# A linear-attention recurrence feeding a bilinear feed-forward block on one core: even tokens scaled by the odd token's alpha, token order restored at the product, one store per block, and new instruction orders

## The chip, the core and the metric

The kernel runs on one core of a Trainium2 chip. The core has a matrix engine (TensorE, "PE"; its weight loads are listed as "PEld"), a vector engine (VectorE, "DVE"), a scalar engine (ScalarE, "ACT"), a general engine (GpSimd, "POOL") and a queue engine (SyncE, "SP"). Each runs its own list of instructions in order and waits on semaphores for the others. 16 DMA engines move data between device memory and the core's on-chip memory; transfers are issued from the SP, POOL and ACT queues. [...]

The metric is the device time of one execution in microseconds (us).

## The reference

Attention first, over 4 batches, 8 heads, 768 tokens and a head width of 48, with one state matrix per batch and head:

```python
for t in range(S):
    state = alpha[:, :, t, :, None] * state + np.einsum('bhd,bhe->bhde', k[:, :, t], v[:, :, t])
    y[:, :, t] = np.einsum('bhd,bhde->bhe', q[:, :, t], state)
```

Its output, 3072 tokens of 384 features, goes through the feed-forward block:

```python
a = x @ w_a          # 384 -> 1536
b = x @ w_b          # 384 -> 1536
return (a * b) @ w_out   # 1536 -> 384
```

## The kernel before, in words

**Tiles.** The work is cut into six chunks. Chunk c holds two batches (units u = 0 and 1) and 256 consecutive tokens of each. A partition holds a pair of neighbouring tokens: r = 0 is the even one, r = 1 the odd one. The pairs split into two groups g of 64 partitions (`HC`).

**Attention of a chunk.** alpha, k, q and v are loaded (`load`). ACT takes the logarithm of alpha (`logs`, line 553), DVE adds the two logarithms of a pair (`pairs`, line 559), and a matmul with a triangular matrix sums them along the pairs of a group (`cum` in chunk 0, `cum2` in the others). The sum is the decay exponent of the odd token. For the even token DVE subtracts the odd token's logarithm (`even`, line 601). `expo` (line 610) makes four exponentials per unit on ACT: beta and its inverse, for odd and for even tokens. DVE multiplies k by the inverse and q by beta (`mul`, line 614). The products are transposed, on PE in chunks 0 and 1 (`turn`, then the copies `turned`), by DMA in the others (`turn_dma`). Then `scores` (line 722), the masking `masked` (line 727) on DVE, the state update (`state_pe`, line 693, and `state`), and the output `inner` and `carried` (both line 738), all in 64x64 tiles. `evac` (line 773) copies a unit's output to `xT`, which holds features on partitions and tokens along the row. Within a block of 128 columns the even tokens come first and then the odd ones.

**Feed-forward of a chunk.** For each of 12 slices f of the hidden width, `ff` (line 789) makes a and b in three matmuls each, for all 512 tokens ("*") or for the 256 of one unit ("0", "1"; `HALVES` takes every other block of 128 columns). ACT copies a out of PSUM (`ff_as`, line 795) and DVE multiplies it by b (`ff_prod`, lines 802 and 805). `ff_o` (line 812) multiplies four blocks m of 128 tokens by w_out, `ff_out` (lines 817 and 819) copies the result, and `store` (line 826) writes it with two DMAs: the 64 rows of even tokens and the 64 of odd ones, each to every other row of the output.

**Order.** Nothing is scheduled automatically. The string `PROGRAM` lists the steps one after another: `chunk: step arguments`. Each engine executes its own steps in that order, so that a waiting instruction holds up everything behind it on its engine, and a DMA waiting at the head of a queue holds up the DMAs behind it. A letter at the end names the engine (V is DVE, S ACT, P POOL, Y SP), a digit the PSUM bank. `K` is state_pe, `k` state, `C` turn, `Ce` turned, `D` scores, `M` masked, `SB` and `SA` carried, `Y` inner, `X` evac, `v` the cast of v, `W` and `Wo` weight loads, `T` turn_dma. `warm` issues matmuls on zeros (line 570) between the first steps. `gate` and `gatet` are one-element copies on POOL that wait for a transfer, so that POOL's loads behind them are issued only then. In chunk 0 the first step of the feed-forward follows the evacuation of unit 0, and the second half of the attention, `Y 1`, comes after it:

```python
0: k 1 1 V; as 1 0; Y 1; SA 1; b 1 0 5; X 1 S; pr 1 0; as 0 0
```

Of the kernel before, what the change touches and what calls it, by code (L numbers as in the profile page):

```python
# [17 lines left out]
0: c1; warm 70 0; cz 0 V; cs 0 V  # L18
0: ld a 0 Y; ld k 0 Y; ld q 0 Y; ld a 1 Y; ld k 1 Y; cs 1 V; ld q 1 Y; gate a 0; ln 0; ld v 0 P; cm 0; cm 1; l2 0 V; A 0 1; warm 48 0; le 0; E 0 b1
0: E 0 i1; cz 1 V; W a 0 256; E 0 i0; W b 0 256; mk 0 V; ln 1; ld v 1 P  # L20
1: ld a 0 P
0: E 0 b0; l2 1 V
1: ld k 0 P
0: mq 0 V; A 1 0
1: ld q 0 P
0: warm 4 1; le 1; E 1 i1
1: ld v 0 P
0: C 0 0 1; dk 6; W a 256 768; E 1 b0; Ce 0 0 V; E 1 i0; W b 256 768; D 0 0 2; E 1 b1; v 0 V; warm 5 4; de; mk 1 V; W a 768 1536; C 0 1 0; K 0 6
0: W b 768 1536; Ce 0 1 S; mq 1 V; warm 11 1
1: ld a 1 P  # L30
0: k 0 0 V; C 1 0 4
1: ld k 1 P
0: M 0 0; SB 0 0
1: ld q 1 P
0: C 1 1 5; Ce 1 0 S
1: ld v 1 P
0: k 0 1 V; D 0 1 2; Ce 1 1 S; Wo 0 6; M 0 1; D 1 0 6; warm 16 4; Wo 6 12; v 1 S; M 1 0
2: ld a * P
0: K 1 4; Y 0; SA 0; k 1 0 V
2: ld k * P  # L40
0: SB 1 6; D 1 1 2; X 0 S; M 1 1
2: ld q * P
1: ln 0
0: a 1 0 0; a 0 0 1
2: ld v * P
0: k 1 1 V; as 1 0; Y 1; SA 1; b 1 0 5; X 1 S; pr 1 0; as 0 0
1: l2 0 V
0: a 5 0 2
1: H 0 S
0: a 3 0 4; as 5 0; a 4 1 5  # L50
1: L 0 V
0: b 0 0 1; as 3 0; a 4 0 6; pr 0 0; a 5 1 7; a 2 0 3; as 4 1; b 5 0 2; b 3 0 0; pr 5 0; b 4 1 4; pr 3 0; as 5 1; b 5 1 2; pr 4 1; as 4 0; b 4 0 7
0: a 2 1 1; as 2 0; pr 4 0; a 1 1 4; pr 5 1; b 2 1 0
1: A2 0 5
0: as 2 1; a 3 1 2
1: le 0; E 0 i1
0: b 3 1 7; b 2 0 6; as 1 1; pr 2 1; a 7 * 3
1: E 0 i0
0: pr 2 0; a 10 * 1; as 3 1
1: mk 0 V; E 0 b1  # L60
0: b 1 1 2; as 10 *; a 6 * 0; pr 3 1; pr 1 1
1: E 0 b0
0: a 0 1 5
1: v 0 V
0: as 7 *; b 11 * 4
1: mq 0 V
0: as 6 *; b 10 * 6; b 7 * 3
1: ln 1
0: pr 10 *; a 11 * 7; pr 7 *; as 0 1; b 6 * 0
1: l2 1 V  # L70
0: as 11 *
1: C 0 0 1
0: pr 6 *
1: H 1 S
0: a 9 * 3
1: Ce 0 0 S; L 1 V
0: b 0 1 2
1: dk 6
0: pr 11 *; as 9 *; pr 0 1
1: D 0 0 4  # L80
0: b 9 * 1
1: de; M 0 0; A2 1 7; C 0 1 6; E 1 i1
0: pr 9 *
1: K 0 2; E 1 b1
0: a 8 * 0
1: k 0 0 V; le 1
0: b 8 * 5
1: k 0 1 V; E 1 b0
0: o 3 0 1; as 8 *
1: mq 1 V; E 1 i0  # L90
0: o 0 0 3; pr 8 *
1: Ce 0 1 S
0: o 2 0 0
1: mk 1 V; SB 0 6; D 0 1 4; C 1 0 2; M 0 1
0: o 0 1 -; o 2 1 -; ot 0 S; o 3 1 -; ot 2 V
1: Ce 1 0 V
0: st 2 Y
1: Y 0; SA 0
0: ot 3 S
1: v 1 V; D 1 0 0  # L100
0: st 3 Y
1: K 1 4; X 0 S; M 1 0; C 1 1 3
2: ln *
1: b 3 0 2; a 1 0 6; Ce 1 1 V; b 11 0 1; a 3 0 0; k 1 0 V
0: o 1 0 7
1: as 3 0
2: l2 * V
1: as 1 0; b 1 0 0; k 1 1 V
0: o 1 1 -
2: H * S  # L110
1: pr 3 0; a 0 0 5; pr 1 0
0: ot 1 S
1: a 11 0 4
2: L * V
1: b 0 0 2; as 0 0; a 5 0 0; as 11 0; a 8 0 3; pr 0 0; as 5 0; SB 1 6; D 1 1 4; pr 11 0; as 8 0; a 4 0 0; M 1 1
2: A2 1 2
1: as 4 0
2: A2 0 1; E 1 i1
1: b 4 0 3; a 2 0 0
2: le 1; E 0 b1  # L120
1: b 5 0 4
2: le 0; E 1 b1
1: b 8 0 5; Y 1; SA 1
2: E 1 i0
1: pr 4 0
2: dec
1: pr 8 0
2: E 0 b0
1: pr 5 0; a 6 0 3; X 1 S
2: mk 1 V  # L130
1: a 7 0 2; a 10 0 5; as 2 0; b 11 1 7
2: mq 0 V; E 0 i1
1: b 2 0 4
0: st 1 Y
1: b 6 0 0; as 7 0; b 7 0 1; as 6 0; pr 2 0; a 9 0 6
2: E 1 b0
1: pr 7 0; a 2 1 3
0: st 0 Y
1: a 0 1 2; pr 6 0; as 10 0; b 10 0 4
2: mq 1 V  # L140
1: as 2 1; b 2 1 0; as 0 1; b 0 1 5
2: v 1 S
1: a 9 1 1; pr 10 0
2: T 1
1: b 9 1 2; pr 0 1; a 5 1 3; as 9 1; pr 2 1; a 4 1 4
2: E 0 i0
1: b 4 1 1; pr 9 1; as 4 1; b 5 1 5
2: mk 0 V
1: a 11 1 0; as 9 0; b 9 0 4; as 5 1; a 3 1 2; pr 4 1
2: T 0  # L150
1: b 3 1 6; pr 9 0; as 3 1; a 1 1 1; pr 5 1; a 8 1 3; as 11 1; b 1 1 4; pr 3 1; as 1 1; a 10 1 0; pr 11 1; as 8 1; b 8 1 6; pr 1 1
2: v 0 S; gatet 1; D 1 0 2
3: ld a * P
1: pr 8 1; a 7 1 1
2: M 1 0
1: as 10 1
2: K * 6
1: as 7 1
3: ld k * P
1: b 6 1 5  # L160
2: k * 0 V
1: a 6 1 3; b 7 1 4
3: ld q * P
1: as 6 1
2: D 0 0 0
1: o 3 0 2
2: k * 1 V
3: ld v * P
1: pr 7 1; b 10 1 6; o 2 0 3; pr 6 1; pr 10 1
2: M 0 0; SB 1 4; D 1 1 6  # L170
1: o 2 1 -
3: ln *
2: M 1 1
1: o 1 0 1; ot 2 S
3: l2 * V
2: Y 1; SA 1
3: H * V
1: o 1 1 -
2: X 1 S
3: L * V  # L180
2: SB 0 6
1: ot 1 S
2: D 0 1 4
1: o 0 0 3
2: M 0 1
1: st 1 Y
3: A2 0 0; A2 1 1; E 0 b1
2: Y 0; SA 0
3: le 1; E 0 i1; le 0; E 1 b1
1: o 3 1 -  # L190
2: X 0 V
3: E 0 i0; dec; E 1 i1
1: o 0 1 -
3: v 0 V; E 1 i0; mk 0 V; E 0 b0
2: a 4 * 7
3: E 1 b0; mq 0 V
2: a 3 * 0
1: st 2 Y
2: a 0 * 5; as 3 *
3: mq 1 V  # L200
2: b 3 * 6
3: T 0
2: as 4 *
3: mk 1 V
2: a 6 * 1
3: v 1 S
2: b 4 * 4; pr 3 *
1: ot 0 S
2: b 0 * 7; as 6 *
1: st 0 Y  # L210
2: pr 4 *; a 1 * 3; as 0 *; b 6 * 6
1: ot 3 S
2: pr 0 *
3: T 1
2: as 1 *; a 9 * 5
1: st 3 Y
2: pr 6 *; b 1 * 2; as 9 *
3: D 0 0 0
2: pr 1 *
3: K * 6; M 0 0  # L220
2: b 11 * 5; b 2 * 2
3: k * 0 V
2: a 11 * 1
3: gatet 1
2: a 2 * 0
4: ld a * P
2: as 11 *
3: k * 1 V
2: b 9 * 4; as 2 *
4: ld k * P  # L230
2: b 7 * 3; pr 9 *; a 7 * 1; pr 11 *
4: ld q * P
2: a 8 * 6; as 7 *; pr 2 *; a 5 * 0
4: ld v * P
2: as 8 *; pr 7 *
3: D 1 0 4
2: as 5 *; a 10 * 7
3: M 1 0
2: b 8 * 1; as 10 *; b 5 * 2; pr 8 *
4: ln *  # L240
3: SB 1 6
2: pr 5 *
3: D 1 1 4
2: b 10 * 0
3: M 1 1
2: o 0 0 2
4: l2 * V
2: o 3 0 3; pr 10 *
4: H * S
3: Y 1; SA 1  # L250
4: L * V
3: SB 0 4; D 0 1 0; X 1 S
2: o 0 1 -
3: M 0 1
4: A2 0 7
2: o 1 0 6; ot 0 V
4: E 0 b1; le 0
2: st 0 Y
3: Y 0; SA 0
4: E 0 b0  # L260
2: o 3 1 -
3: X 0 S
4: E 0 i1; A2 1 0
3: b 11 * 4
4: E 0 i0; le 1
3: a 0 * 2
2: ot 3 V
4: E 1 b0
3: a 11 * 5
4: mq 0 V  # L270
2: o 2 0 1
3: as 11 *
4: mk 0 V
3: as 0 *; b 0 * 3
4: T 0; E 1 i0
2: o 2 1 -
3: pr 0 *
4: E 1 i1; v 0 S; mk 1 V
2: o 1 1 -
4: E 1 b1  # L280
3: a 7 * 5
2: ot 2 S
4: mq 1 V
3: b 7 * 3
4: v 1 S
2: st 2 Y
3: pr 11 *; a 8 * 0
2: ot 1 S
3: a 5 * 1
4: T 1  # L290
3: as 7 *; b 8 * 2
4: dec
3: pr 7 *; as 5 *
4: D 0 0 6
3: a 3 * 5
4: M 0 0
3: a 2 * 1; as 3 *; b 5 * 3
2: st 1 Y
3: as 8 *; b 2 * 7; pr 5 *
2: st 3 Y  # L300
3: b 3 * 4; pr 8 *; as 2 *
4: gatet 1
5: ld a * P
3: a 1 * 6; pr 3 *; a 4 * 5; pr 2 *; as 1 *
5: ld k * P
3: b 1 * 4; as 4 *; b 4 * 2; pr 1 *
5: ld q * P
4: K * 6
3: pr 4 *; a 6 * 3
5: ld v * P  # L310
4: k * 0 V
3: b 6 * 1; as 6 *
4: D 1 0 4
3: pr 6 *
4: SB 1 2; D 1 1 6
3: a 10 * 0
4: M 1 0
3: a 9 * 1; as 10 *
4: M 1 1
3: b 10 * 5; as 9 *; b 9 * 4  # L320
5: ln *
3: o 2 0 1; pr 9 *; pr 10 *
4: SB 0 6; Y 1; SA 1
5: l2 * V
4: D 0 1 4
3: o 0 0 0
4: X 1 S; M 0 1
5: H * S
3: o 0 1 -
5: L * V  # L330
4: Y 0; SA 0
5: A2 1 2
4: X 0 S
3: o 2 1 -
5: le 1; E 1 i1
3: ot 0 V
4: a 4 * 7
5: E 1 i0; E 1 b0
4: b 6 * 6
5: mk 1 V; E 1 b1; A2 0 0  # L340
4: a 6 * 5
3: ot 2 V
5: E 0 b1
4: b 3 * 3
5: dec
4: as 6 *; a 3 * 1; as 4 *; pr 6 *; a 1 * 5; as 3 *
5: mq 1 V
4: b 4 * 6; as 1 *
5: le 0
4: b 1 * 1  # L350
5: T 1; E 0 i1
4: pr 4 *; a 7 * 2
5: E 0 i0
# [60 lines left out]
5: as 9 *; b 2 * 2; as 6 *; b 9 * 6; a 2 * 7; pr 9 *
# [506 lines left out]
```

## Time and profile before

| | before |
|---|---|
| time, median of 3 runs | 210.22 us (208.12 to 212.03) |
| profiled execution: first to last instruction | 207.3 us |
| PE busy, matmuls | 192.6 us, 2702 |
| PE weight loads | 121.6 us, 2718 |
| DVE busy | 139.9 us |
| ACT busy | 101.2 us |
| POOL busy | 38.0 us |
| DMA | 29.42 MB, 52587 packets |
| chain that ended last | PE 53%, issue 24%, DMA 9%, DVE 6% |

The profiled execution's own time is its span: its last store lands at 206.3 us and its last instruction ends at 207.3 us. The three timed runs are other executions, and lie 0.8 to 4.7 us above it. A matmul's busy time overlaps the next one's, so PE's busy share says that PE had something in flight, not that it streamed at its full rate. Rates are read from the starts of consecutive matmuls: 38 matmuls of 512 columns take 8.37 us in the chain from 169.3 us on, which is 0.22 us each.

### The profile page before, as it was taken

The page shows a single profiled execution, that of the slowest core. Times are in us where ns is not written, and L with a number is a line of the kernel's source. Part 1 is how long each engine was busy: PE and PEld are TensorE (multiplying, and loading weights), DVE is VectorE, ACT ScalarE, POOL GpSimd, SP SyncE. Part 2 cuts the span into 40 slices and gives each one's busy share as a digit, 9 for nine tenths or more (in the row PEclk, how much of TensorE's full clock was granted, in tenths as well). Part 3 has the DMA queues.
Part 4 walks back from the last instruction along what each step waited for, and adds up shares of the span by engine and source line. Part 5 has one row for each costly group of instructions (what it writes and reads, how often), then busy time and mean ns, then how long its engine had stood idle before and what let it go on. Part 6 is the DMA issues. An engine that isn't in the chain of part 4 may idle for free.

```text
span 207.3 us, 6249 instructions
## 1 busy us (share of the span) xinstructions
PE 192.6 (93%) x2702; PEld 121.6 (59%) x2718; DVE 139.9 (67%) x223; ACT 101.2 (49%) x192; POOL 38.0 (18%) x54
## 2 busy tenths in 40 slices
PE   8988499999999989999998899999999999999991
PEld 8867378575778866564545554456545554454560
DVE  5799435887599979579885766698597755423530
ACT  3456344874378850567342576535683344332200
POOL 3896636000000027000080000530000000000000
PEclk9999859999999999999999999999999999999998
DMA  6999999999310697997959919699457200004155
GB/s 163 239 238 246 207 243 232 225 276 215 55 39 4 110 173 198 257 123 141 179 141 263 152 33 196 72 280 263 41 83 145 61 3 0 0 0 112 38 120 112
DMA packets 52587, 29.42 MB, mean 142 GB/s; under 512 B 42760, under 2 KB 49672, under 8 KB 52560
## 3 DMA queue, kind: packets, MB, share of 16 engines
q0 software_dynamic: 19552, 17.70, 45.5%
q1 hardware_dynamic: 33008, 11.33, 28.1%
q8 instruction: 21, 0.34, 0.6%
q14 instruction: 6, 0.05, 0.1%
HBM read 25.98 MB, written 4.74 MB: 148 GB/s over the span
## 4 chain that ended last, share of the span: by engine, by line
PE 53%; issue 24%; DMA 9%; DVE 6%; ACT 4%; POOL 2%; POOLq 0%; ACTq 0%; DVEq 0%
PE psum L789 28%; PE psum L812 15%; DMA a_t<-in_alpha_dram 7%; PE psum L738 4%; DMA kqT<-QKp 2%; ACT la L553 1%; DVE l L559 1%; PE psum L722 1%; PE psum L693 1%; ACT kqT L660 1%; PE psum L574 1%; PE psum L596 1%; DVE S L518 1%; DVE vx L513 1%; DVE m L727 1%
## 5 line engine op out<-in xcount | busy, mean ns | idle before, releaser
L789 PE MATMUL psum<-xT,wa_t 128*128 128x512 bf16 (+1 forms) x262 | 57.2, 344 | 1.3 <-ACT xT L773 0.6
L789 PE MATMUL psum<-xT,wb_t 128*128 128x512 bf16 (+1 forms) x262 | 56.4, 338 | 0.6 <-issue 0.5
L812 PE MATMUL psum<-wo_t,prod 128*128 128x384 bf16 x288 | 51.5, 326 | 0.1
L812 PEld LDWEIGHTS <-prod 128*128 128x128 bf16 x288 | 27.2, 98 | 19.3 <-issue 0.3
L789 PEld LDWEIGHTS <-wa_t 128*128 128x128 bf16 x270 | 26.2, 101 | 20.4 <-issue 0.9
L789 PEld LDWEIGHTS <-wb_t 128*128 128x128 bf16 x270 | 25.8, 99 | 19.9 <-issue 0.3
L727 DVE TENSOR_TENSOR m<-psum,mask 128x1024 bf16<-128x1024 f32 x24 | 29.0, 1220 | 7.9 <-PE psum L722 7.7
L839 POOL CAST go<-kqT 1x1 f32<-1x1 bf16 x3 | 0.5, 173 | 83.9 <-DMA kqT<-QKp 83.9
L773 ACT ACTIVATE xT<-psum 128x768 bf16<-128x768 f32 x11 | 8.9, 808 | 14.4 <-PE psum L738 14.3
L817 ACT ACTIVATE ot<-psum 128x384 f32<-128x384 f32 x13 | 6.4, 492 | 18.2 <-PE psum L812 18.2
L553 ACT ACTIVATE la<-a_t 128x768 f32<-128x768 f32 (+1 forms) x8 | 9.3, 1165 | 11.6 <-DMA a_t<-in_alpha_dram 11.6
L738 PE MATMUL psum<-m,vx 64*64 64x128 bf16 x576 | 10.9, 221 | 2.8 <-issue 2.5
L722 PE MATMUL psum<-kqT 64*64 64x128 bf16 x384 | 10.3, 219 | 2.7 <-DVE prod L802 1.7
L738 PEld LDWEIGHTS <-vx 64*64 64x64 bf16 x576 | 8.9, 109 | 6.1 <-issue 6.1
L570 PE MATMUL psum<-wz 128*128 128x128 bf16 x154 | 11.2, 238 | 1.0 <-DVE one L493 1.0
L614 DVE TENSOR_TENSOR QKp<-k_t,invb 128x768 bf16<-128x768 f32 x12 | 11.4, 953 | 0.9 <-ACT invb L610 0.9
L570 PEld LDWEIGHTS <-wz 128*128 128x128 bf16 x154 | 10.3, 108 | 1.9 <-DVE one L493 1.0
L614 DVE TENSOR_TENSOR QKp<-q_t,beta 128x768 bf16<-128x768 f32 x12 | 11.3, 951 | 0.0
L722 PEld LDWEIGHTS <-kqT 64*64 64x64 bf16 x384 | 7.2, 106 | 5.3 <-issue 3.8
L819 DVE COPY ot<-psum 128x384 f32<-128x384 f32 x11 | 6.0, 553 | 6.0 <-PE psum L812 6.0
L601 DVE TENSOR_TENSOR le<-psum,la 128x384 f32<-128x384 f32 x12 | 6.5, 553 | 5.0 <-PE psum L596 3.7
L559 DVE TENSOR_TENSOR l<-la 128x384 f32<-128x384 f32 (+1 forms) x8 | 6.0, 746 | 4.7 <-ACT la L553 4.7
(244 smaller groups left out, 261.3 us busy)
## 6 DMA issues: line engine op xcount, KB each, us to landing
out_dram<-ot SPq DMA_DIRECT2D x48, 96.0 KB, 2.2
a_t<-in_alpha_dram POOLq DMA_DIRECT2D x4, 768.0 KB, 7.8
k_t<-in_k_dram POOLq DMA_DIRECT2D x4, 768.0 KB, 9.7
q_t<-in_q_dram POOLq DMA_DIRECT2D x4, 768.0 KB, 11.4
v_t<-in_v_dram POOLq DMA_DIRECT2D x4, 384.0 KB, 12.4
wo_t<-in_moe_w_out_dram POOLq DMA_DIRECT2D x2, 576.0 KB, 16.0
a_t<-in_alpha_dram SPq DMA_DIRECT2D x2, 384.0 KB
k_t<-in_k_dram SPq DMA_DIRECT2D x2, 384.0 KB, 6.9
```

The lines of the kernel that those rows point to most:

```text
L553: nc.scalar.activation(out=ch.la[:, us].rearrange("p b h r d -> p (b h r d)"), in_=ch.a[:, us].rearrange("p b h r d -> p (b h r d)"), func ...
L559: eng.tensor_add(ch.l2[:, us].rearrange("p b h d -> p (b h) d"), x[:, :, 0, :], x[:, :, 1, :])
L570: nc.tensor.matmul(w[:, :C], lhsT=wz, rhs=wz, start=True, stop=True)
L601: nc.vector.tensor_sub(ch.le[:, u], ch.pf[u].rearrange("p (h d) -> p h d", h=H), ch.la[:, u, :, 1, :])
L614: eng.tensor_mul(QKp[ch.c % 2][:, u, j, :, :, :D], src[:, u].rearrange("p h r d -> p r h d"), by[:, :, u])
L722: nc.tensor.matmul(s2[g * HC:(g + 1) * HC, r, p, rk, :], lhsT=ch.kqT[u][rs, 1, rk, 2 * h + p, g * HC:(g + 1) * HC], rhs=queriesT(ch, u, 2 ...
L727: nc.vector.tensor_mul(m.rearrange("p r a k s -> p (r a) (k s)"), ch.s2[u, h].rearrange("p r a k s -> p (r a) (k s)"), maskn(4))
L738: nc.tensor.matmul(y[c * DP:(c + 1) * DP, g, j // 2 * C:(j // 2 + 1) * C], lhsT=lhsT, rhs=rhs, start=(g, c) not in begun, stop=False, skip ...
L773: nc.scalar.activation(out=o_, in_=i_, func=AF.Copy)
L789: nc.tensor.matmul(p, lhsT=(wa_t, wb_t)[w][:, kk, f * 128:(f + 1) * 128], rhs=ch.xT[:, kk, us, :], start=(kk == 0), stop=(kk == KT - 1))
L812: nc.tensor.matmul(op, lhsT=ch.prod[:, f, m * C:(m + 1) * C], rhs=wo_t[:, f, :], start=(f == 0), stop=(f == NFF - 1))
L817: nc.scalar.activation(out=ot, in_=ch.pf["o", m], func=AF.Copy)
```

## The change

**Even tokens.** The four exponentials and the subtraction `even` go. Instead, k of the even token is multiplied in place by the odd token's alpha, and q of the even token by its inverse `ra`, which ACT makes from the logarithm (`ratio`, `level`). The same beta and inverse then serve both tokens of a pair. Of the 24 `level` multiplications 9 run on DVE and 15 on POOL.

**Token order.** `xT` now holds a unit's two blocks side by side. `ff_prod` writes its product with a step of two elements, so that even and odd tokens stand in their true order, and `store` writes a block of 128 rows with one DMA.

**Start.** The 154 small filler matmuls become 35 with 512 columns (`fill`). The zeroing of the padded tiles moves from DVE to POOL and covers only the padding. k of unit 0 is loaded from POOL's queue at once, and both gates go. Of chunk 1's loads, most follow the first weight loads. Chunk 0's first eight half-width feed-forward groups precede `Y 1`.

**Last block.** Block 1 of chunk 5 is made in two halves of 192 columns (`ff_oc`, `ff_outc`, `store_part`), the last of them copied on ACT and stored from ACT's queue.

**Orders.** `PROGRAM` is new throughout: steps of neighbouring chunks interleave differently, some loads of alpha, k and q move from POOL's queue to SP's, and the decay rows (`decay_rows`, `decay_load`) are written and read back in two separate steps.

```diff
 PROGRAM = """
-0: c1; warm 70 0; cz 0 V; cs 0 V
-0: ld a 0 Y; ld k 0 Y; ld q 0 Y; ld a 1 Y; ld k 1 Y; cs 1 V; ld q 1 Y; gate a 0; ln 0; ld v 0 P; cm 0; cm 1; l2 0 V; A 0 1; warm 48 0; le 0; E 0 b1
-0: E 0 i1; cz 1 V; W a 0 256; E 0 i0; W b 0 256; mk 0 V; ln 1; ld v 1 P
-1: ld a 0 P
+0: c1; ld a 0 Y; ld k 0 P; cz 0 b P; c1a; cu; cu2 P; cm 0; fill 7 6; fill 1 0; cz 0 q P; ld a 1 Y; ln 0; l2 0 V; lv 0 k V; ln 1; fill 1 3; ld v 0 P; ld q 0 Y
+0: ra 0; fill 2 4; fill 11 0; fill 4 0; A 0 1; l2 1 V; ra 1; E 0 i; cm 1; ci; cs 0 m P; cz 0 v P; fill 3 6; dk 5; ld v 1 P; ld k 1 Y; E 0 b; fill 1 2; A 1 0
+0: lv 0 q V; cz 1 q P; mk 0 V; mq 0 V; ld q 1 Y; lv 1 k P; de; E 1 i; C 0 1 5; C 0 0 2; E 1 b; v 0 V; W a 256 768; K 0 6; W a 0 256; mk 1 V; Ce 0 0 S; k 0 0 V
+0: lv 1 q P; Ce 0 1 S; D 0 0 3; fill 5 6; W b 0 256; W b 256 768; SB 0 0
+1: ld a 0 P
+0: v 1 S; M 0 0; D 0 1 4; mq 1 V; M 0 1; K 1 2
...
+0: Y 0; Ce 1 0 S; k 1 0 V; SA 0; D 1 0 5; C 1 1 2; k 1 1 V; X 0 S; Ce 1 1 S; M 1 0; c2 V; a 3 0 1; a 5 0 4; D 1 1 2; SB 1 6; a 1 0 5; as 5 0; as 1 0; W b 768 1536
+0: M 1 1; a 0 0 4; a 2 0 0; as 3 0; b 1 0 5; b 3 0 2; b 5 0 3; pr 5 0; pr 3 0
+0: Y 1; as 2 0; SA 1; X 1 S; pr 1 0
...
+5: oc 1 1 0 5; oc 1 0 0 6; o 2 0 2; pr 7 *; oc 1 0 1 -; o 3 1 -; o 0 0 7; o 0 1 -; ot 3 V; o 2 1 -
+5: ot 0 S; oc 1 1 1 -; otc 1 0 V; stc 1 0 Y; st 3 Y; ot 2 V; otc 1 1 S; st 0 Y; st 2 Y; stc 1 1 S
...
-    HALVES = (slice(0, B, 2), slice(1, B, 2))
+    HALVES = (slice(0, 2), slice(2, 4))
...
+    def fill(n, i):
+        for _ in range(n):
+            nc.tensor.matmul(bank(i), lhsT=wz[:, :C], rhs=wz, start=True, stop=True)
...
-    def even(ch, u):
...
-        nc.vector.tensor_sub(ch.le[:, u], ch.pf[u].rearrange("p (h d) -> p h d", h=H), ch.la[:, u, :, 1, :])
+    def ratio(ch, u):
...
+        nc.scalar.activation(out=ch.ra[:, u], in_=ch.la[:, u, :, 1, :], func=AF.Exp, scale=-1.0)
+
+    def level(ch, us, what, eng):
+        t, by = (ch.k, ch.a[:, us, :, 1, :]) if what == "k" else (ch.q, ch.ra[:, us])
+        for u in range(us.start, us.stop):
+            x = t[:, u, :, 0, :]
+            eng.tensor_mul(x, x, by[:, u - us.start])
...
-        o_ = ch.xT[:, :, u::2, :].rearrange("p a g s -> p g a s")
+        o_ = ch.xT[:, :, 2 * u:2 * u + 2, :].rearrange("p a g s -> p g a s")
...
+    def tokens(x, us):
+        return x.rearrange("p (b s r) -> p b r s", s=HC, r=2)[:, us]
+
+    def columns(x, n):
+        return x.rearrange("p (b r s) -> p b r s", r=2, s=HC)
...
+        o_, a_, b_ = tokens(ch.prod[:, f, :], us), columns(a[:, :n], n), columns(b, n)
+        nc.vector.tensor_mul(o_, a_, b_)
...
+    def rows_of(ch, m):
+        row = (ch.b0 + m % 2) * S + (2 * ch.s + m // 2) * C
+        return out[row:row + C, :]
+
     def store(ch, m, eng):
...
-        for r in range(2):
-            eng.dma_start(out=rows[r], in_=ch.ot[m][r * HC:(r + 1) * HC])
+        eng.dma_start(out=rows_of(ch, m), in_=ch.ot[m])
+
+    def store_part(ch, m, h, eng):
+        eng.dma_start(out=rows_of(ch, m)[:, part(h)], in_=ch.ot[m][:, part(h)])
```

## The prediction

> **What bounds the kernel now.** The page first: PE has something in flight nearly always, and its clock is full but for two slices.
>
> ```profile
> PE 192.6 (93%) x2702; PEld 121.6 (59%) x2718; DVE 139.9 (67%) x223; ACT 101.2 (49%) x192; POOL 38.0 (18%) x54
> ...
> PEclk9999859999999999999999999999999999999998
> ...
> q8 instruction: 21, 0.34, 0.6%
> ```
>
> Next, busy time in four stretches of my choosing (columns: stretch, its length, busy us of PE, PEld, DVE, ACT, POOL, granted clock, DMA share, GB/s).
>
> ```profile
> 0.00:22.00 22.00, 18.81 (x448) 16.56 (x449) 17.16 (x32) 10.77 (x18) 15.87 (x32) 1.00 1.21 221
> 22.00:32.00 10.00, 7.25 (x85) 5.24 (x85) 3.40 (x7) 3.75 (x9) 4.39 (x5) 0.66 1.17 233
> 32.00:203.00 171.00, 166.50 (x2172) 99.78 (x2185) 119.36 (x185) 86.14 (x165) 17.75 (x18) 1.00 0.67 127
> 203.00:207.30 4.30, 0.00 (x0) 0.00 (x0) 0.00 (x0) 0.49 (x1) 0.00 (x0) 0.81 0.46 103
> ```
>
> From 32 us on PE sets the pace: 166.5 of 171 us busy, at full clock. What can be won lies in the first 32 us, where the feed-forward hardly begins, and in the last 4.3. So third, PE's timeline from 20 to 28 us.
>
> ```profile
> 22.27 0.81 PE L789 MATMUL psum<-xT,wa_t 128*128 128x256 bf16 x6 [0.64 <-ACT xT L773]
> 23.01 0.58 PE L738 MATMUL psum<-m,vx 64*64 64x128 bf16 x25
> 26.07 0.85 PE L738 MATMUL psum<-m,vx 64*64 64x128 bf16 x23 [2.48 <-issue]
> 26.71 0.53 PE L738 MATMUL psum<-kqT,Sm 64*64 64x128 bf16 x6
> ```
>
> Y of unit 1 stops half-way, 25 of 48 matmuls in, and waits 2.48 us for nothing that the profile shows. Then the clock is halved: the clock records have 0.5 from 24.8 to 31.6 us. I read the wait as PE's own instruction fetch. 5,420 PE instructions over the 21 packets of q8 are 258 each; the two "issue" waits inside the small matmuls (0.45 us at 20.15, 2.48 at 26.07) stand 256 instructions apart; and a packet of q8 runs from 23.75 to 24.69 us, inside the second. A stretch of 64x64 tiles uses up a packet in 3 to 4 us (20.15 to 23.4 here), and with the DMA share above 1 the next was not there.
>
> [...]
>
> **The change at the start.** I compare both kernels where Y of unit 1 runs. Walk of the new order, with durations of this trace:
>
> - alpha of unit 0 has landed at 4.6, as now (ACT L553 starts at 4.66, 0.84 us). The pair sum starts at 5.55 and not at 6.29, because the zeroing of S and Sm (3.77 to 6.37 on DVE) is gone. It ends at 6.1.
> - The fillers undo that. 26 of 512 columns stand before the first triangular matmul. A full-clock one costs 0.22 us (38 in 8.37 us from 169.3 on) and twice that until the clock rises at 4.3: 8 by then and 18 x 0.22 = 4.0 after, so 8.3 us. The matmul runs 8.3 to 9.2, 1.4 us later than now.
> - `even` (0.56) and one exponential are off the chain, so k's product starts at 9.2 + 0.49 = 9.7 (now 9.75), q's ends at 11.6, and the sixteen transposes are done at 12.5. Even.
> - POOL is what comes next. Its steps up to the load of v of unit 1 end at 10.2 us, counted from 0.75: two loads and two masks by their rows (0.9, 1.0, 1.7, 1.35 us), zeroing at 0.11 us plus 0.8 ns an element (from 0.14 for 64 and 0.32 for 256 elements: 0.95, 1.4 and 0.5), identity and triangle 1.3, gaps. Now that load is issued at 10.51 and the cast of v follows 16.9; by the same 6.4 us v lands at 16.6, its cast on ACT (0.84) ends at 17.5, then state matmuls 0.33, transposes 0.5, Y of unit 0 with its carried part 0.9, evacuation 0.81: 20.2 us, where now it is 22.2.
> - Eight half-width groups (24 matmuls, 0.11 us each) then run before Y of unit 1. They need four weight loads, of which the last (w_b, columns 256 to 768) lands at 26.3 now, behind 1.57 MB of chunk 1's loads. 1.18 MB of these now go behind it, 1.35 us per 0.39 MB by the landings: 22.2; issued late by POOL, at 16.5, it may be 24. The last groups end, and Y of unit 1 starts, at 24.0.
>
> Against now: 26.07 - 24.0 = 2.1 us earlier; minus 0.4 for the 25 matmuls of Y already done now; plus 18 more matmuls done (24 against 6) x 0.11 = 2.0; plus the half-clock work from 26.07 to 31.63, 5.6 / 2 = 2.8 if the clock holds. Sum **6.5 us**. The fetch wait goes since the block of 256 that holds Y of unit 1 now begins with it and the block before it holds 24 wide matmuls, 4.7 us of PE work and about 7 us of time. What is late next are w_b's last columns (32 now, 31.7 by the same landing rates, needed at 33) and k of chunk 1's unit 0, about 33, whose `level` stands on DVE ahead of products due from 32 on: I charge 0.7 us.
>
> **POOL's multiplications.** No row shows one. From below, DVE's 0.54 us for the same 128x384 f32; from above, 1.2 us, POOL's mask select (L504, 0.81 us for 256 elements) scaled to 384. I take 1.0, nearer POOL's own row; two of them precede w_b's load, so the ends move 24.0 by -0.9 to +0.4. [...]
>
> **From 32 us on.** PE's matmuls (L789, L812, L738, L722, L693) are the same in number and shape, so what a new order can win there is PE's idle time: 4.5 us by the window row, 1.7 of it one wait at 113 us for a product on DVE. DVE loses 12 subtractions of 0.55 and gains 9 multiplications of 0.54: -1.7 us, hidden behind PE except in dense stretches (9.14 of 10 us at 100 to 110). ACT loses 24 of 48 exponentials and gains 12 ratios: 12 x 0.5 = -6 us, hidden, ACT being at half load. POOL gains 15 us and stays idle most of the time; but k, q and some loads now wait behind each other on it. Without the gates a transpose by DMA (4.3 us to landing) can meet a load of 768 KB (2.9 us at the landing rate of 84.1 to 87.1), so up to 3 us late per chunk where PE has no other work; it has the previous chunk's groups. Denser stretches of small tiles in the new order (256 instructions with 3.3 to 4 us of PE work, three times) could meet the fetch again: 0 to 2 us each. I set gains and losses equal, 0, with -4 to +4 for the range.
>
> **The product's step of two.** [...] Taken at 0; from above a doubling, which is the third rival.
>
> **The end.** Now PE ends at 203.0, a copy of 384 columns (0.49), two stores issued one after the other (0.47 and 0.59), landing at 206.3. After it: a copy of 192 columns (0.32, from 0.38 for 256), one store from ACT's own queue, 2.1 us to landing like now; SP's last whole block lands about as late, 2.6 after PE's end against 3.3. **0.7 us.**
>
> **Sum.** 207.3 - 6.5 + 0.7 - 0.7 = 200.8 us for a profiled execution. The median of the runs lies 2.9 above the profile's span; I keep that distance: **203.7 us**.
>
> **Rivals.**
> - *The clock drops earlier* (0.20). While PE waits for the cast of v, from 15.4 to 17.5 us, it has only five fillers before and small tiles around, about 1.35 us of work in 3.5; now the drop at 24.8 followed a stretch with about 1.1 in 3.4. For it: similar shares. Against it: the stretch from 14.6 to 18.0 now, with its small fillers, holds 2.7. Half a clock for 6.8 us over some 5 us of work costs 4: 204.8 + 2.9, **207.7 us**.
> - *The order wins more* (0.17). PE's 4.5 us of idle time after 32 us go, most of them: **199.5 us**.
> - *DVE becomes the bound* (0.08, the other side). The 90 products write with a step; if that doubles them (0.69 to 1.2, 0.42 to 0.7), DVE gets 38 us more, 2.7 per 10 us from 60 on, where rows of 7.7 to 9.1 then need 10.4 to 11.8. Excess over twelve such stretches 7 us, with PE waits for banks about 14: **214.8 us**. It decides from +0.4 us a product, where it eats the 6.5. [...]
> - *The wait at 26 us is no fetch and stays* (0.10, the change not doing at its place what I say): 2.1 + 2.0 - 0.4 remain, **206.5 us**.
> - The forecast itself: 0.45.
>
> **How the numbers follow.** About 2% (4.2 us) is what a measurement here can tell from no change, so the bounds are 206.0 and 214.4. Faster: 0.42 of the forecast's 0.45, 0.17, 0.04 of the clock's 0.20, 0.04 of the fetch's 0.10: 0.67. Slower: 0.05 of DVE's 0.08 and 0.04 for a clash of queues that I don't see: 0.09. Same: 0.24. The range takes in the better order and the clock's drop with a little each side: 198.5 to 209.0; left out are DVE's case and the tails, near 0.17.
>
> **What would show it.** Right: Y of unit 1 of chunk 0 starts near 24 us without an "issue" wait of microseconds, a granted clock of 1.00 from 22 to 32 us, PE's last matmul near 196.6, multiplications on POOL near 1.0 us, the product still 0.69 us, the end 3.6 us behind PE. Wrong: a product above 0.9 us, a clock of 0.5 before 25 us, PE waiting on loads between 25 and 45 us, or new "issue" waits at 45 us or later.

## The result, and the profile after

| | before | after |
|---|---|---|
| time, median | 209.17 us (206.80 to 212.03, 4 runs) | 201.85 us (200.93 to 202.41, 4 runs) |
| profiled execution: span | 207.3 us | 200.0 us (its run took 201.8) |
| PE busy, matmuls | 192.6 us, 2702 | 189.6 us, 2594 |
| DVE, ACT, POOL busy | 139.9, 101.2, 38.0 us | 137.5, 97.5, 52.6 us |

The changed kernel is faster: ratio **0.968, 95% interval 0.960 to 0.976**. Ratios leave out executions more than 1.5% slower than the fastest one of the same kernel. 203.7 us were predicted, with a range of 198.5 to 209.0. The total is right, but two of its large terms are not. The page of the changed kernel, cut to the lines shown of before:

```profile
PE 189.6 (95%) x2594; PEld 114.8 (57%) x2611; DVE 137.5 (69%) x209; ACT 97.5 (49%) x182; POOL 52.6 (26%) x68
...
PEclk9996999999999999999999999999999999999999
...
q8 instruction: 20, 0.33, 0.7%
```

PE's clock falls once, near 16 us, and no longer near 28. The same in four stretches (columns: stretch, its length, busy us of PE, PEld, DVE, ACT, POOL, granted clock, DMA share, GB/s):

```profile
0.00:22.00 22.00, 17.26 (x297) 9.80 (x299) 13.38 (x18) 9.59 (x16) 20.18 (x38) 0.92 1.17 212
22.00:32.00 10.00, 9.43 (x156) 7.73 (x150) 7.76 (x17) 7.42 (x16) 7.06 (x9) 1.00 1.11 242
32.00:196.00 164.00, 162.26 (x2148) 96.84 (x2161) 115.82 (x174) 80.12 (x152) 25.34 (x23) 1.00 0.68 133
196.00:200.00 4.00, 0.63 (x7) 0.40 (x5) 0.56 (x1) 0.33 (x1) 0.00 (x0) 0.97 0.36 123
```

From 22 to 32 us PE is busy for 9.43 us at full clock; before it was 7.25 at 0.66. From 32 us on it has nothing in flight for 164.0 - 162.26 = 1.7 us, against 4.5 before. Third, PE's timeline where Y of unit 1 of chunk 0 runs (L750 with 48 matmuls):

```profile
25.35 0.82 PE L804 MATMUL psum<-xT,wb_t 128*128 128x256 bf16 x6
26.44 0.49 PE L804 MATMUL psum<-xT,wb_t 128*128 128x256 bf16 x3 [0.27 <-issue]
26.86 0.86 PE L750 MATMUL psum<-m,vx 64*64 64x128 bf16 x48
27.56 0.33 PE L750 MATMUL psum<-kqT,Sm 64*64 64x128 bf16 x6
```

The 48 matmuls run through: the 2.48 us wait in their middle is gone, and a boundary of 256 instructions just ahead of them costs 0.27 us. But they start at 26.86 us, not near 24.0. The reason stands on DVE, from 9 to 16 us:

```profile
10.14 0.96 DVE L623 TENSOR_TENSOR QKp<-k_t,invb 128x768 bf16<-128x768 f32 x1 [0.45 <-ACT invb L619]
11.02 2.61 DVE L623 TENSOR_TENSOR QKp<-q_t,beta 128x768 bf16<-128x768 f32 x1
13.55 2.02 DVE L691 COPY vx<-v_t 128x768 bf16<-128x768 bf16 x1
```

and on POOL at the same time:

```profile
11.79 1.00 POOL L612 TENSOR_TENSOR k_t<-k_t,a_t 128x384 f32<-128x384 f32 x1
12.74 1.57 POOL L530 DMA_DIRECT2D wa_t<-in_moe_w_a_dram  x2
14.33 1.01 POOL L612 TENSOR_TENSOR q_t<-q_t,ra 128x384 f32<-128x384 f32 x1
15.27 1.57 POOL L530 DMA_DIRECT2D wb_t<-in_moe_w_b_dram  x2
```

A product of the same shape takes 0.96 us in one line and 2.61 in the next, and the cast of v 2.02 us, where its fastest on DVE takes 0.35. Both lie beside POOL's multiplications (L612) and DMA issues. PE starves behind them (1.44 and 1.09 us of waits), and its clock is 0.5 from 15.44 to 18.85 us.

So the 7.3 us are made up like this, by the prediction's own way of counting: **start 3.6** (Y of unit 1 0.8 later instead of 2.1 earlier, -0.4, +2.0, +2.8), **from 32 us on 2.8** (4.5 - 1.7), **end 0.9** (PE ends at 196.63, 3.4 before the end of the span; before it was 202.99, 4.3 before). That is 7.3.

The half clock that the +2.8 stands for does not come in every execution of the kernel before. Of 25 executions on record beside the experiments, four had a clock of 1.00; they took 206.65 to 207.55 us.

### The profile page after: what moved, and what is told of

Read it like the earlier page. It is cut to its first block, busy times and chain, and to the rows that moved or that the text cites. A ratio compares the mean times of both kernels' runs of the same rounds, so it can differ in the third digit from the quotient of the medians.

```text
span 200.0 us, 6005 instructions
## 1 busy us (share of the span) xinstructions
PE 189.6 (95%) x2594; PEld 114.8 (57%) x2611; DVE 137.5 (69%) x209; ACT 97.5 (49%) x182; POOL 52.6 (26%) x68
## 4 chain that ended last, share of the span: by engine, by line
PE 88%; DVE 6%; issue 3%; ACT 2%; ACTq 0%; DVEq 0%
PE psum L804 44%; PE psum L826 22%; PE psum L750 7%; PE psum L571 5%; PE psum L734 3%; DVE QKp L623 3%; PE psum L601 2%; PE psum L705 2%; PE psum L666 1%; DVE vx L691 1%; PE psum L837 1%; ACT invb L619 1%; DVE prod L818 1%; DVE m L739 1%; ACT kqT L672 1%
## 5 line engine op out<-in xcount | busy, mean ns | idle before, releaser
L804 PE MATMUL psum<-xT,wa_t 128*128 128x512 bf16 (+1 forms) x261 | 54.4, 335 | 1.5 <-DVE prod L818 0.6
L826 PE MATMUL psum<-wo_t,prod 128*128 128x384 bf16 x276 | 50.4, 327 | 0.1
L826 PEld LDWEIGHTS <-prod 128*128 128x128 bf16 x276 | 25.7, 98 | 18.2 <-issue 0.5
L612 POOL TENSOR_TENSOR q_t<-q_t,ra 128x384 f32<-128x384 f32 x9 | 9.3, 1038 | 82.3 <-ACT ra L606 47.1
L623 DVE TENSOR_TENSOR QKp<-q_t,beta 128x768 bf16<-128x768 f32 x12 | 14.2, 1186 | 1.0 <-POOL k_t L612 0.8
L841 ACT ACTIVATE ot<-psum 128x384 f32<-128x384 f32 (+1 forms) x12 | 5.8, 480 | 15.0 <-PE psum L826 14.0
L843 DVE COPY ot<-psum 128x384 f32<-128x384 f32 (+1 forms) x13 | 6.7, 537 | 8.8 <-PE psum L826 8.8
L571 PE MATMUL psum<-wz 128*128 128x512 bf16 x33 | 10.6, 479 | 1.5 <-DVE one L485 1.2
L672 ACT ACTIVATE kqT<-psum 128x1024 bf16<-128x1024 bf16 x8 | 8.0, 1023 | 8.2 <-PE psum L666 8.1
L750 PE MATMUL psum<-m,vx 64*64 64x128 bf16 x576 | 10.6, 217 | 0.6 <-DVE m L739 0.6
L750 PEld LDWEIGHTS <-vx 64*64 64x64 bf16 x576 | 9.0, 107 | 2.1 <-issue 2.0
L619 ACT ACTIVATE invb<-psum 128x384 f32<-128x384 f32 x12 | 5.9, 493 | 5.4 <-PE psum L601 3.1
```

The lines of the kernel that those rows point to most:

```text
L571: nc.tensor.matmul(bank(i), lhsT=wz[:, :C], rhs=wz, start=True, stop=True)
L612: eng.tensor_mul(x, x, by[:, u - us.start])
L619: nc.scalar.activation(out=t[:, u].rearrange("p h d -> p (h d)"), in_=ch.pf[u], func=AF.Exp, scale=sc)
L623: eng.tensor_mul(QKp[ch.c % 2][:, u, j, :, :, :D], src[:, u].rearrange("p h r d -> p r h d"), by[:, u].rearrange("p (o h) d -> p o h d", o ...
L672: nc.scalar.activation(out=o_, in_=i_, func=AF.Copy)
L750: nc.tensor.matmul(y[c * DP:(c + 1) * DP, g, j // 2 * C:(j // 2 + 1) * C], lhsT=lhsT, rhs=rhs, start=(g, c) not in begun, stop=False, skip ...
```

## The experiments

Steps of `PROGRAM` are shown cut out of their lines. All ratios are to the kernel before, with 95% intervals.

**1. Is the wait in Y of unit 1 a fetch?** In the kernel before, 20 of 48 small fillers became 5 wide ones, so that PE has 30 instructions fewer ahead of chunk 0's attention.

```diff
-0: warm 48 0
+0: warm 28 0; fill 5 0
```

> The kernel before, with 20 of the 48 small fillers behind the first triangular matmul replaced by 5 of 512 columns: the same columns, 30 PE instructions fewer ahead of the attention. Fetch theory: the block boundary moves 30 instructions later, so the long 'issue' wait in Y of unit 1 stands after 40 of its 48 matmuls instead of 25, still 1.5 to 3 us. Data theory (the wait is for something that lands late): it stays after 25 of 48, or is tied to a landing. Time 205 to 212 us either way.

Measured: 213.42 us in one run, above the 205 to 212 expected. PE's timeline:

```profile
22.00 0.26 PE L697 MATMUL psum<-vx,QKp 64*64 64x48 bf16 x4 [2.18 <-issue]
...
27.93 0.43 PE L742 MATMUL psum<-m,vx 64*64 64x128 bf16 x8 [0.45 <-issue]
```

Both waits moved by the instructions taken out: the one in Y of unit 1 now stands after 40 of 48 matmuls instead of 25 (15 matmuls with their weight loads are 30 instructions), the other after 26 state matmuls of unit 1. The place goes with the count of instructions and not with the work, so the wait is PE's fetch. The sizes changed places: the long one is now at the earlier boundary (2.18 us), the short one in Y (0.45). Both kernels show a similar time from one block to the next. By the count of instructions the boundary before these two was crossed at 15.15 us here and at 14.70 in the kernel before. From one crossing to the first instruction behind the next boundary it took 5.45 and 5.92 us before, and 6.85 and 5.93 here, each time with a packet of q8 that starts 2.9 to 4.1 us after the crossing. In these four cases the next block of 256 was usable only after that time, and PE waited for the rest where it had used up the one before sooner: in 3.4 us before Y's wait of 2.48, in 4.7 us here before the 2.18.

**2. What do the gates cost before?** The three gates that hold back POOL's loads until a transpose has landed are taken out of the kernel before.

```diff
-2: gatet 1
-3: gatet 1
-4: gatet 1
```

> The kernel before without its three gates on the DMA transposes, nothing else. If the gain after 32 us comes from loads that start earlier: the wait of 1.7 us at 113 us goes, PE's idle time after 32 us falls from 4.5 to 2 to 3 us, time 1 to 2.5 us shorter than before. If transposes and loads collide instead: PE waits 2 us or more on kqT, time the same as before or longer.

Measured: 219.95 us (218.81 to 222.94), ratio 1.049 (1.041 to 1.058). What PE waited for, in total us, times, longest:

```profile
PE psum L720 <- DMA kqT<-QKp: 9.9, 3, 5.5
PE psum L736 <- issue: 2.5, 1, 2.5
```

The transposes come late behind the loads, by up to 5.5 us. The gates were worth some 11 us in their order. The changed kernel has none and waits for no transpose, so what replaces them is its order of loads and transposes on SP and POOL.

**3. Does a boundary inside Y of unit 1 suffice for the wait?** Each wide filler of the changed kernel became four small ones, 210 PE instructions more.

```diff
-0: fill 7 6
+0: warm 28 6
...
```

> The changed kernel with each wide filler replaced by four of 128 columns: the same columns at the same places, 210 PE instructions more ahead of the attention. Fetch theory: boundaries fall into Y of unit 0 (17th matmul) and Y of unit 1 (21st); 'issue' waits of 0.5 to 2.7 us there, perhaps a half clock behind them; 203 to 206 us. If wide fillers matter only as PE time: no such waits, 201 to 202.5 us like the changed kernel.

Measured: 202.54 us (199.67 to 203.29), ratio 0.970 (0.963 to 0.977). By the count of instructions two boundaries fell into dense small tiles, one of them into this line, and neither shows a wait:

```profile
23.87 0.86 PE L750 MATMUL psum<-m,vx 64*64 64x128 bf16 x48
```

PE took 5.0 and 5.9 us for the two blocks ahead of them (13.29 to 18.27 to 24.18), and the packets came early enough (14.38 and 21.41). So a boundary in dense work alone made no wait: with 5.0 and 5.9 us of work ahead of it there was none, with 3.4 us (the kernel before) and 4.7 us (experiment 1) there were 2.48 and 2.18 us. The width of the fillers itself makes no difference that can be measured.

**4. Is it POOL that slows DVE at the start?** The two multiplications for unit 1 of chunk 0 go to DVE.

```diff
-0: lv 1 k P
+0: lv 1 k V
...
-0: lv 1 q P
+0: lv 1 q V
```

> The changed kernel with chunk 0's two level multiplications of unit 1 on DVE instead of POOL. [...] Landing theory (v of unit 1 and the weights set the pace anyway): Y of unit 1 starts less than 0.7 us earlier, 201 to 202.4 us.

Measured: 199.53 us (199.38 to 201.22), ratio 0.955 (0.949 to 0.962). DVE's timeline in the same place:

```profile
12.00 0.95 DVE L623 TENSOR_TENSOR QKp<-q_t,beta 128x768 bf16<-128x768 f32 x1
12.87 0.55 DVE L612 TENSOR_TENSOR k_t<-k_t,a_t 128x384 f32<-128x384 f32 x1
13.34 0.35 DVE L691 COPY vx<-v_t 128x768 bf16<-128x768 bf16 x1
```

Product and cast have their short times again, and the clock does not fall after the start. In this execution it rose only at 7.19 us instead of 5.19, so the triangular matmul came 1 us later, and two fetch waits stand ahead of Y of unit 1:

```profile
18.75 0.55 PE L666 MATMUL psum<-ident,QKp 128*128 128x128 bf16 x7 [1.09 <-issue]
25.22 0.49 PE L804 MATMUL psum<-xT,wb_t 128*128 128x256 bf16 x3 [0.40 <-issue]
```

Y still starts 1.2 us earlier, at 25.64, where the landing theory had less than 0.7. DVE has two instructions more and is done sooner.

**5. Then all 15 on DVE?**

```diff
-1: lv 0 q P
+1: lv 0 q V
...
```

> The changed kernel with all 15 level multiplications of POOL moved to DVE. DVE gets 15 x 0.54 = 8 us more work, POOL loses 15 x 1.0. Theory (what POOL's multiplications cost is the slowing of DVE beside them, and only chunk 0 has no cover for it): the start gains as in the run with chunk 0's two on DVE, q's product of unit 0 near 0.95 and the cast of v below 0.6 us; the later 13 change little, since DVE has slack behind PE: 199.0 to 201.0 us, PE's idle time from 32 us on within 1 us of the changed kernel's 1.7. Rival (DVE is near its limit after 45 us, and POOL's relief of it is what the middle gained): at least 3 of the extra 7 us come back as waits of PE for DVE's products, 202.5 to 206 us.

Measured: 226.66 us (225.22 to 228.21), ratio 1.085 (1.075 to 1.096). Both theories missed, by 20 us and more. The start was as good as the theory had it (Y of unit 1 at 23.57). What was lost lies later, DVE first:

```profile
110.61 0.56 DVE L612 TENSOR_TENSOR q_t<-q_t,ra 128x384 f32<-128x384 f32 x1 [13.85 <-DMA q_t<-in_q_dram]
```

PE, at the same time, waits for a copy that stands behind it on DVE:

```profile
111.69 0.19 PE L705 MATMUL psum<-vx,QKp 64*64 64x48 bf16 x1 [13.78 <-DVE ot L843]
```

And this is the same multiplication on POOL in the changed kernel:

```profile
102.25 1.00 POOL L612 TENSOR_TENSOR q_t<-q_t,ra 128x384 f32<-128x384 f32 x1 [13.93 <-DMA q_t<-in_q_dram]
```

It waits 13.9 us for its load there too, and nobody notices, since next behind it on POOL stand a load and a multiplication of the next chunk, and PE waits for neither. Experiment 12 takes this one alone.

**6. What are the product's order and the single store worth?** The product is written contiguously again, and each block goes out with two DMAs.

```diff
-        o_, a_, b_ = tokens(ch.prod[:, f, :], us), columns(a[:, :n], n), columns(b, n)
...
+        for r in range(2):
+            eng.dma_start(out=rows[r], in_=ch.ot[m][r * HC:(r + 1) * HC])
```

> The changed kernel with the product written contiguously again and each block stored by two DMAs of alternate rows as in the kernel before; the other parts stay. Theory (the reordering write costs 0.02 to 0.03 us a product, hidden, and the second store only issue time on SP, 0.5 us each): product 0.69 and 0.42 us, DVE 2 us less busy, time within 1 us of the changed kernel, 201 to 203 us; the end 0.3 to 0.6 us later, since the last whole blocks' stores are twice as many on SP. Rival (one store per block is worth something in the middle, through fewer DMAs ahead of the weight loads and transposes): 203.5 us or more, with PE waiting on DMAs.

Measured: 203.34 us (201.87 to 204.62), ratio 0.973 (0.962 to 0.984). A product of 256 columns takes 0.42 us here and 0.44 in the changed kernel, one of 512 0.68 and 0.73 on average, so writing with a step costs 0.02 to 0.04 us. The end of the span, on SP's queue:

```profile
196.19 3.96 SPq L860 DMA_DIRECT2D out_dram<-ot  x6
```

Six issues take SP until 200.15 us. PE ends at 197.58 and the span at 202.7, so 5.1 us lie behind PE instead of 3.4. The single store is worth 1.7 us at the end, three times what was expected; in the time, 1.5 us, with overlapping intervals. PE itself ends 0.9 us later as well, and waits for a transpose, which it does not do in the changed kernel:

```profile
PE psum L734 <- DMA kqT<-QKp: 0.8, 1, 0.8
```

So the rival, a gain in the middle too, is not excluded.

**7. The changed orders without the scaling.** Four exponentials and the subtraction again, no ratio, no multiplication by it; chunk 5's logarithm stands behind chunk 4's last exponential.

```diff
+        even(ch, u)
+        for r in (1, 0):
+            src = ch.pf[u] if r else ch.le[:, u].rearrange("p h d -> p (h d)")
...
```

> The changed kernel with the even tokens done as before: DVE subtracts, ACT makes four exponentials a unit, no ratio and no multiplication by it; everything else, the orders too, stays (chunk 5's logarithm moves behind chunk 4's last exponential). POOL loses 15 us, ACT gains about 12 x 0.5 = 6 us, DVE 1.7 us. Theory 1 (the scaling is worth its place at the start: two operations off the chain to k's product, 0.56 + 0.5 us, but its collision with DVE costs 1.2 to 2 us there): Y of unit 1 of chunk 0 within 1 us of 26.9, time 200.5 to 202.5 us, so no gain from this part as it is placed. Rival (the scaling itself brings a good part of the 7 us, by relief of ACT and DVE): 203.5 to 206 us, with ACT or DVE among what PE waits for from 32 us on.

Measured: 219.26 us (216.33 to 221.32). Both theories missed the time by 13 us and more; Y of unit 1 starts at 27.12, as theory 1 had it. Busy time from 60 to 70 and from 80 to 90 us, columns as above:

```profile
60.00:70.00 10.00, 7.51 (x123) 5.50 (x121) 7.09 (x13) 6.91 (x17) 0.00 (x0) 1.00 0.02 4
80.00:90.00 10.00, 3.90 (x57) 2.41 (x56) 4.19 (x8) 0.25 (x1) 0.00 (x0) 0.68 1.32 209
```

In the changed kernel PE is busy for 10.0 and 9.95 us there. DVE's subtraction now stands between the triangular matmul and ACT's exponentials. ACT waits 9.6 us in all for it. The exponentials end later, the products too, the second transpose is issued at 75.1 us instead of 69.4, lands behind other transfers, and PE waits 6.09 us for it at 87.28. These orders have no room for the old chain: the scaling isn't a small extra of this change but what its orders stand on. Orders written for four exponentials were not tried.

**8. What is the split of the last block worth?** The last block is made whole.

```diff
-5: oc 1 1 0 5; oc 1 0 0 6
+5: o 1 0 5
...
-5: otc 1 0 V; stc 1 0 Y; otc 1 1 S; stc 1 1 S
+5: ot 1 S; st 1 Y
```

> The changed kernel with the last block of chunk 5 made whole: twelve matmuls of 384 columns into one bank, one copy of 384 columns on ACT, one store on SP; the rest stays. Theory (the split wins by its shorter copy and by a store that does not queue behind SP's others): PE's end to the end of the span 4.2 us against 3.4, time about 0.8 us longer, 202.3 to 203.0 us. Rival (the split's twelve extra matmuls and its dependence on an extra bank take that back): within 0.3 us of the changed kernel.

Measured: 200.03 us (199.91 to 202.37), ratio 0.960 (0.951 to 0.970), span 198.1. PE ends at 194.61, 3.5 us before the span does, against 3.4 with the split: the theory falls, the split is worth 0.1 us. By experiment 6 the gain at the end comes from the single store.

Up to its last block this is the changed kernel's program, and so its profile shows the start of that program once more:

```profile
10.72 0.95 DVE L623 TENSOR_TENSOR QKp<-q_t,beta 128x768 bf16<-128x768 f32 x1
11.59 1.47 DVE L691 COPY vx<-v_t 128x768 bf16<-128x768 bf16 x1
```

The clock rises at 4.58 us instead of 5.19, the first triangular matmul starts at 8.47 instead of 8.77, the product of q is through at 11.67, before POOL begins at 11.81; the clock stays at 1.00, and Y of unit 1 starts at **23.94**. This start has two outcomes. Four profiles have it: experiment 12's is like this one (clock up at 4.56, product 0.95 us, Y at 23.92), experiment 6's like the changed kernel's (clock up at 5.49, product 2.47 us, clock 0.5 from 15.73 on, Y at 26.62).

**9. The two edits together.** Chunk 0's two multiplications on DVE and the last block whole.

> The changed kernel with chunk 0's two multiplications for unit 1 on DVE and with the last block whole. Theory (DVE's slowing beside POOL was the start's loss, and the split of the last block brings nothing): the two add up to little more than the first alone, 198.5 to 200.0 us, a clock of 0.996 or more in nearly every execution. Rival (both of the earlier gains were only the clock not falling at 15 us by chance): 200.5 to 202 us, the clock at 0.991 in about half of the executions.

Measured: 199.35 us (198.98 to 202.68, 6 runs), ratio **0.957 (0.950 to 0.964)**. The span of the profile is 197.8 us, Y of unit 1 starts at 24.18 though the clock rose only at 6.88. The mean granted clock was 0.997 or more in five of six executions; in the changed kernel it was 0.991 in three of four, and 0.998 in the one that took 200.93 us. Over all executions with the changed kernel's start (its own and those of experiments 6 and 8) it was 0.991 or less in six of twelve, with the two multiplications on DVE (experiment 4 and this one) in one of ten. That speaks against the rival, chance alone, but the count is small. The interval still meets that of the changed kernel at its edge, so the 2.5 us between the medians are likely, not certain.

**10. What bounds the start now?** The same without 11 wide fillers ahead of the first triangular matmul.

```diff
-0: fill 2 4; fill 11 0; fill 4 0
+0: fill 2 4; fill 4 0
```

> The kernel of the run before with 11 of the 26 wide fillers that stand ahead of the first triangular matmul taken out: that matmul can start up to 2.4 us earlier, at 7.5 us or before instead of 8.5 to 9.8. Theory (from 22 us on the start waits for the landing of w_b's columns 256 to 768, near 22, so that an earlier chain of products only makes PE wait there): within 0.5 us of the run before, with PE waiting 1 to 2 us for w_b. Rival (the chain from the first triangular matmul sets Y of unit 1): 1.0 to 2.0 us faster. Third (fewer fillers raise the clock later, or let it fall): 1.5 us slower or more.

Measured: 200.67 us (199.45 to 201.17), ratio 0.961 (0.956 to 0.967): no gain, by the medians 1.3 us more than in the run before, with overlapping intervals. The rival falls; the third isn't excluded, since the mean clock was 0.983 and 0.989 in two of six executions. The triangular matmul started at 6.34 instead of 9.60 us, and Y of unit 1 at 23.95 instead of 24.18. PE's wait in between is not for w_b, as the theory had it, but for the cast of v of unit 1:

```profile
17.17 0.45 PE L705 MATMUL psum<-vx,QKp 64*64 64x48 bf16 x32 [1.54 <-ACT vx L689]
```

That cast waited for its load, landed at 16.25 us. A start 3.3 us earlier ends in a wait for a transfer, only another one than expected.

**11. The scaling alone, in the kernel before.** Even tokens as in the change (on DVE in chunk 0, on POOL behind the loads in the others), all else as before.

```diff
-1: l2 0 V
+1: l2 0 V; ra 0; lv 0 k P; lv 0 q P
...
-1: le 0; E 0 i1
+1: E 0 i
```

> The kernel before with one part of the change alone: even tokens scaled by alpha and its inverse (on DVE in chunk 0, on POOL behind each chunk's loads in the others), two exponentials a unit instead of four, no subtraction; orders, product, stores and fillers of the kernel before. Theory (the scaling alone only takes work from engines that have slack, and up to 1 us off the start's chain; the orders carry the gain): 206.5 to 209.5 us, ACT 6 us less busy. Rival (the scaling is what frees the middle): 205 us or less, with less than half of the 4.5 us in which PE had nothing from 32 us on.

Measured: 210.94 us (209.48 to 211.77), ratio 1.010 (1.002 to 1.019): no gain, rather a loss, and above both ranges. ACT is 5 us less busy (96.2), to no use. k's product starts 0.4 us earlier (9.38), and the fetch wait is where it was:

```profile
27.27 0.85 PE L731 MATMUL psum<-m,vx 64*64 64x128 bf16 x23 [2.48 <-issue]
```

From 32 us to PE's end PE has nothing in flight for 6.6 us, against 4.5 before. Neither the scaling in the old orders nor the new orders without the scaling (experiment 7) gain anything; together they do.

**12. One wait, moved.** In the changed kernel only the multiplication of q of chunk 4's unit 1 goes to DVE.

```diff
-4: lv 1 q P
+4: lv 1 q V
```

> The changed kernel with one single multiplication of 15 moved from POOL to DVE: the one of q of chunk 4's unit 1, which stood on POOL 13.9 us for q's load. Theory (POOL is worth its slower multiplication because nothing stands behind the wait there; all products, masks and copies stand behind it on DVE): DVE waits 10 us or more in one piece near 95 to 110 us, PE 7 us or more, 208 to 216 us, for 0.5 us more of work. Rival (what the run with all 15 on DVE lost was DVE's 8 us of extra work, or many small waits): within 1.5 us of the changed kernel, 201 to 203.5 us.

Measured: 215.02 us (214.11 to 215.92), ratio 1.029 (1.020 to 1.039). DVE, and then PE:

```profile
102.58 0.56 DVE L612 TENSOR_TENSOR q_t<-q_t,ra 128x384 f32<-128x384 f32 x1 [12.65 <-DMA q_t<-in_q_dram]
```

```profile
103.66 0.19 PE L705 MATMUL psum<-vx,QKp 64*64 64x48 bf16 x1 [12.50 <-DVE ot L843]
```

One instruction of 0.56 us, moved from POOL to an engine that does it in half the time, costs 13 us. The theory holds in its place, its size and its numbers.

## Why the prediction was right, and where it was not

**The bound and the fetch wait: right.** PE's first 32 us and its end were the place of what could be won, except for the point on the middle below. Experiment 1 shows that the 2.48 us were a fetch, and the changed kernel has no such wait in Y of unit 1. The size of the block (256) was right. So was its condition, small tiles that use up a block faster than the next one comes (3.4 us of work ahead of the 2.48 us; no wait behind 5.0 and 5.9 us in experiment 3); that full DMAs are what delays the block was not tested. Experiments 1 and 3 give the measure that I lacked, 5.5 to 6.9 us from one boundary to the next block. In the changed kernel the block ahead of Y took 6.4 us (19.78 to 26.17), near the 7 that I gave it, and 0.27 us of wait were left. What sets the 5.5 to 6.9 us wasn't tested. Most boundaries cost little: q8 has 21 packets in the kernel before, and PE had "issue" waits of more than 0.2 us at two boundaries (0.45 and 2.48 us).

**The start: the walk was right, one term was missing.** The walk had Y of unit 1 at 24.0 us; where nothing slowed the product of q it started at 23.94 (experiment 8, the same program so far), with 6.5 us won as worked out. In the profiled execution it started at 26.86. The failing step is "POOL's multiplications": I priced them by POOL's own duration (1.0 us, measured 1.00) and by how much they delay w_b's load, and not by what they do to DVE beside them, which the sum had at nothing. There the price was 1.7 us for the product and 1.7 for the cast, and then the fallen clock. Experiment 4 takes the cause away and gets the short times back. The other profiles agree: where POOL multiplies nothing in chunk 0 (the kernel before, experiments 4, 5, 7, 9, 10 and 11), chunk 0's products took 0.94 to 0.96 us and the cast of v 0.35 to 0.80; where it does (the changed kernel, experiments 3, 6, 8 and 12), the product of q took 0.95 to 2.61 and the cast 1.05 to 2.02. The trace of before had a sign of it: its cast of v on DVE took 0.80 us beside a DMA issue of POOL's (0.91 us); in experiment 11, beside the same issue, the cast took 0.35 and the issue 1.03.

In these runs one of the two is held up beside the other, and it can be either: in experiments 3 and 12 POOL's multiplication took 1.21 and 1.39 us and the product beside it 0.95, in the changed kernel the multiplication 1.00 and the product 2.61. Which one started first does not decide it: in all three runs the product did (in the changed kernel at 11.02 us, the multiplication at 11.79). The 1.66 and 1.67 us lost there are longer than one multiplication (1.00), with POOL's next DMA issues following on. What decides it, and by which mechanism, no run shows.

**The clock falling earlier: half right, as a rival.** It was priced at 4 us for 6.8 us of half clock. It fell at 15.44 us for 3.41 us, in three of four timed executions by their mean clock. It came at the time that the rival gave, but not in its wait: v of unit 1 had landed at 15.30, and what PE waited for until 15.62 was unit 0's cast, slowed on DVE. In the 3.42 us before the fall PE was busy for 1.07, with no gap above 1.44; with the good start of experiment 8 it was 2.66 in the same stretch, and the clock stayed. (The "about 1.1" that the prediction read for the kernel before is 1.55 by its row from 21.39 to 24.80.) POOL is not the only way to such a stretch: in experiment 7, without its multiplications, the clock fell at 15.25 after 1.70 us of work. A clock of 0.5 before 25 us was one of the prediction's own signs of being wrong, and it came true.

**From 32 us on: mis-sized.** I set gains and losses equal, 0, in a range of -4 to +4; it was +2.8. The loss I feared most, transposes behind loads of 768 KB, exists (5.5 us in experiment 2), but not in the new order. What the gain comes from is not one part: the scaling alone has 6.6 us of such idle time (experiment 11), the new orders without it 12.8 (experiment 7, from 32 us to PE's end). Which of the new orders made the difference was not separated.

**The product's step: right.** No run shows the 0 that the sum takes; the runs showed 0.02 to 0.04 us each (on average 0.73 and 0.44 us against 0.68 and 0.42), and the rival of a doubled product is gone. Its 214.8 us is 200.8 + 14 without the 2.9 that the other rivals have; on their scale it is 217.7.

**The end: right in size (0.9 for 0.7) by luck, wrong in reason.** I counted the shorter copy and ACT's queue, which are worth 0.1 us (experiment 8). The single store carries it, being worth 1.7 us with the new tail (experiment 6); the new tail with two stores a block would have been worse than the old one.

**Sum.** A start 2.9 us short and a middle 2.8 us long cancelled, which is luck. The 0.7 charged for w_b's last columns and k of chunk 1 did not come (PE waits for neither), and the end gave 0.2 more: together a span of 200.0 us for 200.8. That PE's end came at 196.63 for a predicted 196.6 proves nothing, since by the prediction's own sum it would be 200.8 - 3.6 = 197.2. The time then lay 1.8 us above the span, not 2.9, which is why 201.85 came out below 203.7. With the good start, experiment 8's profile is 1.9 us shorter than the changed kernel's: of its 2.9 us at the start 0.9 goes at 89.3 us, where PE waits 1.48 us for a product on DVE.

## What to carry to other kernels

Price a step that moves to GpSimd three times: by its own duration (1.00 us here, 0.55 on VectorE), by what VectorE does in the same microseconds (a product of 0.95 us took 2.61), and by the waits that it takes along. An in-order engine with nothing behind it is a good place for an instruction that must wait for a load (13.9 us there cost nothing, on VectorE they cost 13), and a bad place beside a VectorE chain that everything waits for. Before undoing one part of a change whose order of work is written by hand, ask which other parts were placed around it.

## What the runs showed of the hardware

- A 128x768 VectorE product of 0.95 us took up to 2.61, and a copy of 0.35 us up to 2.02, beside GpSimd multiplications and DMA issues (the changed kernel); GpSimd's own multiplication of 1.00 us took 1.21 and 1.39 (experiments 3 and 12) and up to 1.70 (the changed kernel).
- A 128x384 f32 multiplication takes 1.00 us on GpSimd and 0.55 on VectorE (medians in the changed kernel).
- PE's fetch waits at the start (0.27 to 2.48 us) stand 256 instructions apart, and in experiment 1 they moved with the 30 instructions taken out ahead of them. There, with a DMA share of 1.11 to 1.22, the block that PE waited for was usable 5.5 to 7.0 us after the boundary before it (the kernel before and after, experiments 1 and 4), and in the kernel before and after 1.3 to 1.6 us after the end of its packet.
- PE's clock rose between 4.56 us (experiment 12) and 7.19 us (experiment 4) in programs that begin with the same wide fillers, and the first triangular matmul behind them started between 8.46 and 9.76 us. The clock fell to 0.5 for 3.41 us in the changed kernel (15.44 to 18.85) and for 6.83 us in the kernel before (24.80 to 31.63). It does not take one long gap: in the 3.41 us before the fall PE was busy for 1.07 us with no gap above 1.44 in the changed kernel, and for 1.55 us with none above 1.21 in the kernel before.
